# One tuned two-layer kernel on one core: the last x block turned by DMA, half-block closing, late statistics, one value product, and a new order of work

## The chip, the cores and the metric

The kernel runs on one core of a Trainium2 chip. The metric is device time in microseconds (us) of that core. A profile shows one execution; its span is about 2 us shorter than the device time of the same run.

Engines: PE is the matrix engine, DVE is VectorE, ACT is ScalarE, POOL is GpSimd.

## The reference

The same pair of blocks runs twice, on 2048 tokens of width 512. Block A is a spectral filter: a two-dimensional real FFT, a product with complex weights, the inverse. Block B is attention with 32 query heads of width 16 and one shared key and value head.

```python
def _A_ref(x, w_r, w_i):
    X = rfft2(x.astype(float32)); X = X * (w_r + 1j * w_i)
    return irfft2(X, s=(S, D)).astype(bfloat16)

def _B_ref(x, wq, wk, wv, wo):                  # H = 32, Dh = 16, one k and one v
    scores = einsum("bhqd,bkd->bhqk", q, k) * Dh ** -0.5
    o = einsum("bhqk,bkd->bhqd", softmax(scores), v)
    return o.transpose(0, 2, 1, 3).reshape(B, S, H * Dh) @ wo

x = A_x
x = x + _A_ref(layernorm(x), w_r, w_i);  x = x + _B_ref(layernorm(x), wq, wk, wv, wo)
x = x + _A_ref(layernorm(x), w_r, w_i);  x = x + _B_ref(layernorm(x), wq, wk, wv, wo)
```

Written as matrix products with host-made tables, a layer has three phases in the trace: transposed blocks and a column transform, then the filter, then the inverse transform with normalization and keys and values (together the spectral stage), and then the attention.

## The kernel before

The kernel is a list scheduler in Python that runs when the program is built. It keeps a clock for each engine, books a duration for every task, and always emits the action that can start first. The instruction order of each engine is thus fixed before the chip sees it; the engines then only wait for each other.

```python
class Plan:
    ACT_EXP = 908.0; DVE_P1 = 600.0; DVE_PH = 610.0; POOL_PH = 1030.0; POOL_LAG = 2600.0   # booked ns
    def step(self):
        while True:
            for i in self.script.get(self.acts, ()):     # choices forced by SCRIPT, by action number
                self.turns.add(i)
            best = None
            for e, c in zip(self.t, (self.pe_next(), self.act_next(), self.dve_next(), self.pool_next())):
                if c is not None and (best is None or c[0] < best[0]):
                    best, eng = c, e
            ...
```

`SCRIPT` is a packed list of small forced choices: at action number n, take the second candidate of an engine, hold PE a little, or put the pass named below on the other engine. It is the "order". As it goes by action number, an edit that adds or removes tasks shifts everything after it, which matters for reading two of the experiments.

In attention, a score unit is 128 keys by 512 queries of one head. ACT takes units in pairs and computes exact exponentials. DVE takes single units: one scale-and-round pass from the PSUM bank to 16-bit integers (below: a score pass), after which two more integer additions per four units (below: phase passes) complete the approximate exponential. A phase pass goes to GpSimd, or, if GpSimd's queue is over 2.6 us long or the order says so, to DVE:

```python
def close(self, end):
    ...
    for p in range(1, K_PH):
        if last: ...
        elif (max(self.t["POOL"] + self.POOL_PH * len(self.pool), end) - end < self.POOL_LAG) != ("phase" in self.turns):
            self.pool.append(...)          # GpSimd: int64_add on the packed 16-bit values
        else:
            self.ph_fifo.append(...)       # DVE: one integer addition, 128x2048
```

The parts that the change touches: statistics aggregate at once, the normalization has a separate shift, each of four value copies is its own instruction, and a block of queries closes only when its last two head groups are normalized together.

```python
def bn(self, L, key, i, x, n, slot=None):
    ...
    self.nc.vector.bn_stats(st, self.ps(slot) if slot else self.x[:, x[1], x[0], :])
    self.nc.vector.bn_aggr(mv[:, i, :], st)

def v_evac(self, t, slot):
    src = self.ps(slot)[:, 0:64].rearrange("p (r d) -> p r d", r=R)
    for i, v in enumerate(self.VS):                        # 1 + 3 weighted copies
        dst = v[:, 4 * t:4 * t + 4, 0:DH]
        if i == 0:
            self.nc.vector.tensor_copy(out=dst, in_=src)
        else:
            self.nc.vector.tensor_single_scalar(out=dst, in_=src, scalar=self.pw[i - 1], op=ALU.mult)

def done(self, b, slot, end):                              # an attention block is finished
    ...
    rc = p.add("DVE", 260.0, [ev, self.evac[b - 1]], lambda k: em.recip(self, b), lazy=tail)
    mu = p.add("DVE", 600.0, [rc], lambda k: em.mul(self, b), lazy=tail, port=True)
    ...                                                    # last two blocks: transposed by DVE, others by DMA
    if g == 3:
        self.layer.close_rows(qb, ...)                     # projection, new x, next layer's statistics
```

The softmax here doesn't subtract the row's maximum and nothing guards it: scores larger than these inputs give would overflow.

## Time and profile before

| | before |
|---|---|
| device time, median of 6 runs | 1315.18 us (1313.65 to 1315.22) |
| profiled span | 1312.7 us |
| first transpose of x on PE | 7.01 us |
| first, third filter group on DVE (see below) | 33.35, 44.64 us |
| DVE score passes, first layer | 108.10 to 663.91 us |
| third filter group, second layer | 695.65 us |
| DVE score passes, second layer | 758.98 to 1301.29 us |

The times of the score passes are the start of the first and the end of the last.

Start with the page: busy time of each engine (share of the span, number of instructions), and for DVE and ACT the span in 40 slices of 33 us, each digit the busy share in tenths. ACT and DVE are full in the attention slices; the two spectral stages are the dips of ACT at the left and in the middle.

```profile
...
PE 1281.5 (98%) x12986; PEld 433.1 (33%) x12986; DVE 1272.7 (97%) x2277; ACT 1223.3 (93%) x1397; POOL 840.1 (64%) x825
...
DVE  6999999999999999999979999999999999999998
ACT  6488999999999999999954899999999999999996
...
```

The DVE alone, from the third filter group to the first score pass of each layer: busy for 58.8 of 63.5 us, so this stage is limited by DVE too, with 4.7 us of waits.

```profile
...
44.64:108.10 63.46, 58.80 (x158) 1.00 0.07 22
695.65:758.98 63.33, 58.61 (x159) 1.00 0.07 22
...
```

The timeline of DVE at the end of the first spectral stage (columns: start us, length us, engine, line, operation, output and input tiles, shapes; in brackets the idle time in front and what ended it). A statistic starts at 98.25, its aggregate at 98.97 and the next work at 99.07. The last aggregate starts at 101.16, the first apply (the instruction that normalizes a row) 0.99 us later. The four value copies start from 106.84 to 107.23. DVE waits 0.60 us for ACT, then 1.24 and 0.66 us for PE.

```profile
...
98.25 0.69 DVE L1091 BATCH_NORM_STATS2 st<-x_sb 128x6 f32<-128x512 bf16 x1
98.97 0.18 DVE L1092 BATCH_NORM_AGGREGATE mv<-st 128x2 f32<-128x6 f32 x1
99.07 0.66 DVE L1317 TENSOR_TENSOR x_sb<-b_68,x_sb 128x512 bf16<-128x512 f32 x1
...
101.16 0.18 DVE L1092 BATCH_NORM_AGGREGATE mv<-st 128x2 f32<-128x6 f32 x1
101.94 0.17 DVE L1108 SCALAR_TENSOR_TENSOR sb<-mv,sb 128x4 f32<-128x4 f32 x1 [0.60 <-ACT sb L1104]
102.15 1.38 DVE L1115 TENSOR_SCALAR xnt<-x_sb,sb 128x512 bf16<-128x512 bf16 x4
...
106.17 0.75 DVE L1348 TENSOR_SCALAR KA<-b_68,part 128x512 bf16<-128x512 f32 x1 [1.24 <-PE b_68 L1340]
106.84 0.22 DVE L1360 CAST vs_116<-b_67 128x64 bf16<-128x64 f32 x1
...
107.23 0.22 DVE L1362 TENSOR_SCALAR vs_119<-b_67 128x64 bf16<-128x64 f32 x1
108.10 0.69 DVE L1394 TENSOR_SCALAR w_1381<-b_68 128x512 uint16<-128x512 f32 x1 [0.66 <-PE b_67 L1382]
...
```

The timeline of PE at the head: matrix products on zeros run until 6.80 us, and the first transpose is at 7.01.

```profile
...
5.00 0.63 PE L1073 MATMUL b_67<-zero 128*128 128x512 bf16 x1
5.43 0.45 PE L1073 MATMUL b_68<-zero 128*128 128x512 bf16 x1
...
6.80 0.38 PE L1073 MATMUL b_66<-zero 128*128 128x512 bf16 x1
7.01 0.61 PE L1152 MATMUL b_67<-tab_ident,x_sb 128*128 128x128 bf16 x8
...
```

The layer change on DVE: the last score pass, the closing of the last block, and the statistics of four new rows one after the other.

```profile
...
663.23 0.68 DVE L1394 TENSOR_SCALAR w_9868<-b_68 128x512 uint16<-128x512 f32 x1
...
666.18 0.72 DVE L1411 STREAM_TRANSPOSE raw<-b_69 128x512 f32<-128x512 f32 x1 [0.70 <-PE b_69 L1404]
...
669.75 0.70 DVE L1091 BATCH_NORM_STATS2 st<-b_67 128x6 f32<-128x512 f32 x1 [0.99 <-PE b_67 L1310]
...
673.23 0.67 DVE L1091 BATCH_NORM_STATS2 st<-b_69 128x6 f32<-128x512 f32 x1
...
684.71 1.29 DVE L58 TENSOR_TENSOR w_10097<-w_9940 128x1024 bf16<-128x1024 bf16 x2 [2.83 <-ACT w_9940 L1216]
```

### The profile page before, as it was taken

What the parts mean: (1) busy time and instruction counts of PE and PEld (TensorE: products, weight loads), DVE (VectorE), ACT (ScalarE), POOL (GpSimd) and SP (SyncE); (2) the same over time, 40 slices, a digit from 0 to 9 for tenths busy, and PEclk for the clock granted to TensorE, in tenths of its full rate; (3) what the DMA queues carried; (4) which work ended last, traced back from release to release, by engine and by line L of the source; (5) the groups of instructions that cost most, each with busy time, mean ns of one, the idle gap of its engine ahead of it and who ended that gap; (6) DMA issues with size and microseconds to landing.
All of it is one profiled execution on the core that took longest, in us unless ns stands there. A gap on an engine that the chain in (4) does not pass through costs nothing.

```text
span 1312.7 us, 31767 instructions
## 1 busy us (share of the span) xinstructions
PE 1281.5 (98%) x12986; PEld 433.1 (33%) x12986; DVE 1272.7 (97%) x2277; ACT 1223.3 (93%) x1397; POOL 840.1 (64%) x825
## 2 busy tenths in 40 slices
PE   9999999999999999999999999999999999999997
PEld 5642222322232222222256423232222232233222
DVE  6999999999999999999979999999999999999998
ACT  6488999999999999999954899999999999999996
POOL 0005777767777677766720067787777777777775
PEclk9999999999999999999999999999999999999999
DMA  9100000011010100010051000000100010000101
GB/s 294 46 1 1 10 9 10 9 32 19 2 12 12 36 10 10 9 34 17 10 169 41 1 1 9 10 10 9 22 14 10 9 22 14 5 8 11 27 5 25
DMA packets 108722, 33.04 MB, mean 25 GB/s; under 512 B 88352, under 2 KB 107296, under 8 KB 108576
## 3 DMA queue, kind: packets, MB, share of 16 engines
q1 hardware_dynamic: 108288, 30.46, 10.0%
q8 instruction: 101, 1.65, 0.5%
q10 hardware_dynamic: 288, 0.56, 0.1%
q14 instruction: 45, 0.37, 0.1%
HBM read 17.89 MB, written 7.60 MB: 19 GB/s over the span
## 4 chain that ended last, share of the span: by engine, by line
ACT 72%; PE 18%; DVE 10%; issue 1%; DVEq 0%
ACT e_0_84 L1387 3%; ACT e_10_94 L1387 3%; ACT e_13_97 L1387 3%; ACT e_3_87 L1387 3%; ACT e_20_104 L1387 3%; ACT e_4_88 L1387 3%; ACT e_12_96 L1387 3%; ACT e_2_86 L1387 3%; ACT e_8_92 L1387 3%; ACT e_7_91 L1387 3%; ACT e_11_95 L1387 3%; ACT e_18_102 L1387 3%; ACT e_1_85 L1387 3%; ACT e_5_89 L1387 3%; ACT e_15_99 L1387 3%; ACT e_14_98 L1387 3%
## 5 line engine op out<-in xcount | busy, mean ns | idle before, releaser
L1382 PEld LDWEIGHTS <-KB 32*128 32x128 bf16 x2048 | 89.7, 91 | 228.5 <-issue 221.4
L1382 PEld LDWEIGHTS <-KA 32*128 32x128 bf16 x2048 | 86.4, 91 | 238.4 <-issue 231.5
L1404 PEld LDWEIGHTS <-vs_116 128*32 128x32 bf16 x2474 | 99.9, 94 | 93.0 <-issue 87.9
L1404 PEld LDWEIGHTS <-vs_117 128*32 128x32 bf16 x1622 | 96.0, 94 | 64.0 <-issue 60.5
L1404 PEld LDWEIGHTS <-vs_118 128*32 128x32 bf16 x1622 | 70.6, 94 | 70.5 <-issue 65.9
L1404 PEld LDWEIGHTS <-vs_119 128*32 128x32 bf16 x1622 | 68.4, 94 | 64.8 <-issue 61.4
L1398 POOL INT64_ADD w_1382<-w_1381 x1 | 1.0, 1040 | 108.1 <-DVE w_1381 L1394 108.1
L1398 POOL INT64_ADD w_10977<-w_10976 x1 | 1.0, 1038 | 97.2 <-DVE w_10976 L1394 97.2
L1387 ACT ACTIVATE e_6_90<-sa_64 128x1024 bf16<-128x1024 f32 x34 | 39.8, 1172 | 1.0 <-PE sa_65 L1382 1.0
L1091 DVE BATCH_NORM_STATS2 st<-x_sb 128x6 f32<-128x512 bf16 x52 | 35.4, 682 | 4.0 <-DMA x_sb<-in_A_x_dram 3.6
L1387 ACT ACTIVATE e_11_95<-sa_65 128x1024 bf16<-128x1024 f32 x31 | 36.5, 1178 | 0.7 <-PE sa_65 L1382 0.7
L1387 ACT ACTIVATE e_12_96<-sa_65 128x1024 bf16<-128x1024 f32 x31 | 36.9, 1189 | 0.2 <-PE sa_65 L1382 0.2
L1387 ACT ACTIVATE e_2_86<-sa_64 128x1024 bf16<-128x1024 f32 x31 | 36.5, 1178 | 0.4 <-PE sa_64 L1382 0.4
L1387 ACT ACTIVATE e_4_88<-sa_65 128x1024 bf16<-128x1024 f32 x31 | 36.6, 1182 | 0.1
L1387 ACT ACTIVATE e_1_85<-sa_64 128x1024 bf16<-128x1024 f32 x31 | 36.6, 1180 | 0.1
L1387 ACT ACTIVATE e_7_91<-sa_64 128x1024 bf16<-128x1024 f32 x31 | 36.6, 1181 | 0.0
L1387 ACT ACTIVATE e_15_99<-sa_65 128x1024 bf16<-128x1024 f32 x31 | 36.6, 1179 | 0.0
L1387 ACT ACTIVATE e_20_104<-sa_65 128x1024 bf16<-128x1024 f32 x31 | 36.4, 1175 | 0.0
L1387 ACT ACTIVATE e_13_97<-sa_64 128x1024 bf16<-128x1024 f32 x31 | 36.2, 1168 | 0.0
L1387 ACT ACTIVATE e_14_98<-sa_65 128x1024 bf16<-128x1024 f32 x31 | 36.0, 1162 | 0.0
L1387 ACT ACTIVATE e_0_84<-sa_65 128x1024 bf16<-128x1024 f32 x30 | 35.5, 1183 | 0.2 <-PE sa_65 L1382 0.2
L1387 ACT ACTIVATE e_9_93<-sa_64 128x1024 bf16<-128x1024 f32 x30 | 35.1, 1170 | 0.2 <-PE sa_64 L1382 0.2
(4077 smaller groups left out, 6474.8 us busy)
## 6 DMA issues: line engine op xcount, KB each, us to landing
it<-const_IT SPq DMA_DIRECT2D x8, 640.0 KB, 5.6
onw<-on SPq DMA_DIRECT2D x120, 32.0 KB, 1.9
x_sb<-in_A_x_dram SPq DMA_DIRECT2D x4, 512.0 KB, 6.8
out_dram<-x_sb SPq DMA_DIRECT2D x16, 128.0 KB, 1.9
way<-x_sb SPq DMA_DIRECT2D x6, 256.0 KB, 2.2
tab_PH<-const_PH ACTq DMA_DIRECT2D x1, 512.0 KB, 4.9
w_131<-const_FT SPq DMA_DIRECT2D x1, 512.0 KB, 8.8
w_136<-const_FT SPq DMA_DIRECT2D x1, 512.0 KB, 8.4
```

The lines of the kernel that those rows point to most:

```text
L1091: self.nc.vector.bn_stats(st, self.ps(slot) if slot else self.x[:, x[1], x[0], :])
L1382: self.nc.tensor.matmul(o, lhsT=KX[rs, kc * P:(kc + 1) * P], rhs=at.QT[qb][rs, g, :], start=True, stop=True, skip_group_check=True)
L1387: self.wrote("ACT", e, self.nc.scalar.activation(out=e, in_=self.ps(slot), func=ACT.Exp, scale=SCALE))
L1398: self.nc.gpsimd.int64_add(t[p][:, 0:n].bitcast(U64), t[0][:, 0:n].bitcast(U64), DELTA[p] * FOUR)
L1404: self.nc.tensor.matmul(self.ps(slot)[32 * h:32 * h + 32, :], lhsT=V[:, kc, :], rhs=rhs, start=first, stop=last, skip_group_check=True)
```

## The change

The intent is to shorten what is not attention, and to let the last queries of a layer close in two halves, so that part of the layer change runs while attention still fills the engines.

1. The plan knows when x arrives, and the last of the four x blocks comes turned by DMA straight from the input, without PE transposes and ACT copies.
2. The statistics of a tile are aggregated one tile late, the shift of the normalization folds into its apply, and the four value copies become one product with broadcast weights.
3. The last token block is normalized in two row pairs, (0, 2) and (1, 3), and so is the first, which before had the pairs (0, 1) and (2, 3).
4. The last two attention blocks of a layer each take both head parities of half of the queries, so rows 0 and 1 can close while rows 2 and 3 attend.
5. A new `SCRIPT`, with one more kind of choice ("flex": ACT may take evacuations that either engine can do while DVE attends).

```diff
-SCRIPT = ( "0ax00902q00k05h..." )
+SCRIPT = ( "1dm02i02d00g00x..." )                         # cut
@@ Layer
+    DMA_X = {3: 13000.0}
+    PAIRED = (0, 3)
@@ load_x
+        for t in L.DMA_X:
+            for j in range(0, R, 2):
+                self.turned(L, [(t, j), (t, j + 1)], self.xt_v[t, P * j:P * j + 2 * P, :])
@@ bn
-        self.nc.vector.bn_stats(st, ...)
-        self.nc.vector.bn_aggr(mv[:, i, :], st)
+        late.append((i, self.small([6], "st", 8)))
+        self.nc.vector.bn_stats(late[-1][1], ...)
+        L.bn_left[key] = L.bn_left.get(key, n) - 1
+        for j, st in late[:] if L.bn_left[key] == 0 else late[:-1]:
+            self.nc.vector.bn_aggr(L.sb[key][0][:, j, :], st)
+            late.pop(0)
@@ apply
-        self.nc.vector.tensor_scalar(..., scalar1=sb[:, 0, i:i + 1], scalar2=sb[:, 1, i:i + 1], op0=ALU.mult, op1=ALU.add)
+        self.nc.vector.tensor_scalar(..., scalar1=mv[:, i, 0:1], scalar2=sb[:, 0, i:i + 1], op0=ALU.subtract, op1=ALU.mult)
@@ v_evac
-        for i, v in enumerate(self.VS): ...               # four copies
+        self.nc.vector.tensor_tensor(out=self.vs[:, :, 4 * t:4 * t + 4, 0:DH], in0=src.unsqueeze(1).to_broadcast(shape),
+                                     in1=self.vw.to_broadcast(shape), op=ALU.mult)
@@ add_back: output rows
-            for j in range(0, R, w): ... for i, r in enumerate(range(j, j + w)):
+            for rows in ((0, 2), (1, 3)) if t in self.PAIRED else (...): ...
@@ Attention
+        self.halves = {nb - 2: 0, nb - 1: 1}
@@ scores
+            if b in at.halves:
+                q = 256 * at.halves[b]
+                for i, KX in enumerate((self.KA, self.KB)):
+                    self.nc.tensor.matmul(o[:, 256 * i:256 * i + 256], lhsT=KX[rs, ...], rhs=at.QT[qb][rs, g, q:q + 256], ...)
+                continue
@@ done
+        if b in self.halves:
+            ...                                            # normalize 256 queries, then
+            self.layer.close_rows(qb, ..., (2 * hf, 2 * hf + 1))
```

Cut here: booked durations, the bookkeeping of the halves and pairs, and the packed order itself.

## The prediction

> **What bounds the kernel now.** Time before: 1315.18 us; profiled span 1312.7 us. Stages in the windows view:
> - Attention, 115-660 and 767-1300 us, 82% of the span: per 20 us ACT is busy 19.9-20.0, DVE 19.5-20.0, GpSimd about 15.5. Score units are shared: 0.917 us of ACT per two units (start to start), 0.60 us of DVE per unit, together 3.85 units/us. A microsecond of DVE work here is worth 0.43 us, of ACT 0.57 us.
> - First spectral stage, 0-108 us. Its head is a chain x, transpose, ACT copy, product, ACT scaling, DVE radix steps; from 33 to 107 us DVE is the limit (18.8-19.6 of 20).
> - Layer change, 664-759 us: the same, entered through the projection of the last rows.
> - Tail, 1301.4-1312.7 us.
>
> **What the change moves.**
> 1. Head. x is there at 4.77 us (first statistics), but PE transposes at 6.80 us, behind dummy matmuls that start every 0.43 us until 5.4 us, then every 0.22 us (as the Trainium skill, "TensorE: Matmul & The Clock Gate", Part 1, gives for cold and warm). The new plan knows this: -1.8 us. Turning the last x block by DMA removes two transposes of 0.45 us and two ACT copies of 0.9 us. Against it, DMA share is 1.0-1.2 until 22 us, and a later DMA transpose of this size takes 3.1-3.7 us to land; weights come later, but not too late. The first filter (33.35 us) should start 2.5-3.5 us earlier.
> 2. DVE in both spectral stages. Statistics now cost 0.79-0.80 us a tile because the aggregate waits for its own tile; one tile late saves about 0.11 us, 16 times per stage after 33 us: 1.7 us. Four value copies take 0.52 us per block, one product an estimated 0.33: 0.8 us. The shift (0.15 us, 5 per stage) goes: 0.7 us. Sum 3 us on a DVE-limited chain, twice.
> 3. Last token block in pairs: at 101-108 us DVE idles 0.6, 1.24 and 0.66 us. Pairs should win 1-1.5 us, twice.
> 4. Halves: the last two blocks each take half of the queries, so rows 0 and 1 close while rows 2 and 3 attend. At the layer change two first products (0.87 us each), a transposition pair, two statistics and half of the normalization leave 666-679 us: 4-5 us shorter, but about 2.6 us of ACT and 2 us of DVE move into attention, costing about 2.4 us. Net -2. Tail: half normalization -1.1 us, two additions fewer -1.2, part paid back: -1.8 us. Score matmuls become twice 256 columns; those start every 0.11 us, so PE should not care.
> 5. New order: attention is full already, about 0.
>
> Sum: head -3, DVE -6, pairs -2.4, layer change -2, tail -1.8, attention -0.5: -15.7 us; I discount it a little.
>
> **Predicted: 1301 us, 8 in 10 between 1293 and 1310.** Faster by over 2%: 0.07; within 2%: 0.91; slower by over 2%: 0.02.
>
> **What would show it.** First transpose near 5 us; first filter near 30 us; first DVE score pass near 100 us instead of 108.1; the gap between last and first DVE score pass at the layer change 95 -> about 86 us; tail 2 us shorter; attention windows unchanged.
>
> **What would make it wrong.** DMA transposes landing after 20 us or delaying filter weights; halves starving the score banks, so that ACT or DVE idles in the last blocks; savings that turn into PE waits; a new order that packs worse.

## More of the kernel before

A filter group is DVE's work on one set of transformed columns: additions of the transform, the product with the complex weights, and more additions. The groups serve as milestones in both traces; the first is dated by its first addition, the third by its first product.

Next the busy time of the engines in the two attention stretches, from the first to the last DVE score pass (columns: stretch, its length, then busy us and number of instructions of each engine, TensorE clock, DMA share, GB/s). DVE is busy 552.51 of 555.81 us and ACT 554.82: an attention stretch has two full engines and no slack.

```profile
...
core 0: us, PE busy (x) PEld busy (x) DVE busy (x) ACT busy (x) POOL busy (x), PEclk, DMA share, GB/s
108.10:663.91 555.81, 548.04 (x5754) 162.58 (x5754) 552.51 (x941) 554.82 (x615) 414.54 (x408) 1.00 0.09 17
758.98:1301.29 542.31, 534.92 (x5726) 159.62 (x5726) 540.42 (x903) 541.51 (x592) 421.16 (x406) 1.00 0.07 12
...
```

## The result and the profile after

| | before | after |
|---|---|---|
| device time, median of 6 runs each | 1315.18 us (1313.65 to 1315.22) | 1307.79 us (1307.62 to 1307.81) |
| ratio | | 0.9946, 95% interval 0.9933 to 0.9959 |
| profiled span | 1312.7 us | 1305.9 us |

A ratio is the mean time of one kernel's fast runs over that of the other's of the same rounds, so it is not quite the ratio of the medians quoted. The change is 7.4 us (0.5%) faster, the class is "same within 2%"; the time is inside the predicted range and 6.8 us above the predicted value. Only 7.4 of the 15.7 us of the prediction's sum came, so the range held by its width (1310 was its upper end), not because the sum was right. The kernel before varies by 1.6 us from run to run, so differences of less than that between two single profiles are weak evidence alone.

The milestones of the two traces cut the span into seven stretches. I use the third filter group, not the first, to end the head; the reason is given below.

| stretch | before | after | difference | predicted |
|---|---|---|---|---|
| head, to the third filter group | 44.64 | 41.46 | -3.18 | -3 |
| first spectral stage, to the first score pass | 63.46 | 61.90 | -1.56 | -4.2 |
| attention 1 | 555.81 | 559.60 | +3.79 | +1.9 for both |
| layer change, to the third filter group | 31.74 | 28.48 | -3.26 | -4.4 |
| second spectral stage | 63.33 | 60.09 | -3.24 | -4.2 |
| attention 2 | 542.31 | 544.77 | +2.46 | (see above) |
| tail | 11.41 | 9.60 | -1.81 | -1.8 |
| span | 1312.70 | 1305.90 | -6.80 | -15.7 |

In the last column the sums of the prediction are laid on the stretches: DVE -3 and pairs -1.2 for each spectral stage; the halves as -4.4 in the layer change and +2.4 in attention, against which the -0.5 stood.

The attention stretches are again full on both engines, but longer. DVE does 4.24 us more work in the first (556.75 against 552.51), GpSimd 6.24 us less (408.30 against 414.54). That hides a shift: ACT runs 599 and 595 score exponentials in the two stretches, against 597 and 592 before, and DVE 804 and 812 score passes against 806 and 816. At 0.917 us from start to start (measured before), two and three more exponentials are 1.8 and 2.8 of the 3.4 and 3.2 us by which ACT's busy time grew. One of them in each stretch is there because ACT had begun 24 exponentials, not 25, before DVE's first score pass.

```profile
...
103.36:662.96 559.60, 548.43 (x5850) 164.74 (x5881) 556.75 (x951) 558.25 (x618) 408.30 (x398) 1.00 0.09 17
751.53:1296.30 544.77, 535.02 (x5819) 163.76 (x5844) 541.98 (x906) 544.69 (x595) 415.35 (x400) 1.00 0.07 12
...
```

Part of what DVE does more is phase passes that the new order gives to it. This is their share of the same two stretches (count in brackets); the kernel before has none there.

```profile
...
103.36:662.96 559.60, 6.48 (x8) 1.00 0.09 17
751.53:1296.30 544.77, 2.75 (x4) 1.00 0.07 12
...
```

A phase pass on DVE has no fixed price. Among the 14 of this kernel, those of 128x2048 16-bit values that began with GpSimd quiet took 0.68 to 0.70 us (the tier table of the Trainium skill's "VectorE: DVE Perf Modes" has 693 ns for such an instruction on bf16 values, which agrees). Two took 1.24 us, each begun while a GpSimd addition had 0.7 us left to run, and two took 1.58 us, begun together with one. The Trainium skill, "GPSIMD Engine Reference", § 1, Specifications, says that GpSimd shares SBUF interfaces with VectorE and that they contend with DVE instructions in a 2-port mode. The trace agrees that they contend: in each of the four cases DVE seems to wait out the running GpSimd instruction (1.04 us) and then take 0.55 us. The two timelines of the kernel after around such a case, DVE first (GpSimd's first addition began at 405.57, 0.34 us ahead; its line is two additions merged):

```profile
...
405.91 1.24 DVE L1471 TENSOR_SCALAR w<-w 128x2048 uint16<-128x2048 uint16 x1
...
```

```profile
...
405.57 2.48 POOL L1469 INT64_ADD w<-w  x2 [2.91 <-DVE w L1465]
...
```

DVE from the third filter group to the first score pass: busy time fell by 2.1 us in the first stage (58.80 to 56.67) and by 2.3 us in the second. The waits (length minus busy) went from 4.66 to 5.23 us in the first and from 4.72 to 3.75 us in the second.

```profile
...
41.46:103.36 61.90, 56.67 (x141) 1.00 0.08 23
691.44:751.53 60.09, 56.34 (x143) 1.00 0.08 23
...
```

The end of the first spectral stage. The aggregates no longer wait, four copies became one product of 0.42 us. The pairs removed one of the three waits: the first apply now follows the last aggregates at once (97.27), and the 0.60 us for ACT are gone, because ACT makes the second pair's factors while DVE applies the first pair's. In the second layer the same wait of 0.60 us is gone too. The two waits for PE stayed (1.46 and 0.70 us against 1.24 and 0.66). PE did not get the first pair any earlier: DVE took the second pair's statistics first and then ran all four applies in one go.

```profile
...
97.05 0.30 DVE L1150 BATCH_NORM_AGGREGATE mv<-st 128x2 f32<-128x6 f32 x2
97.27 1.35 DVE L1169 TENSOR_SCALAR xnt<-x_sb,mv,sb 128x512 bf16<-128x512 bf16 x4
...
101.43 0.75 DVE L1415 TENSOR_SCALAR KA<-b,part 128x512 bf16<-128x512 f32 x1 [1.46 <-PE b L1407]
102.24 0.42 DVE L1425 TENSOR_TENSOR vs<-b,vw 128x256 bf16<-128x256 f32 x1
103.36 4.59 DVE L1465 TENSOR_SCALAR w<-b 128x512 uint16<-128x512 f32 x7 [0.70 <-PE sa L1453]
...
```

ACT in the same time: the last step to each pair's factors. The first pair's were ready at 95.61, 1.66 us before DVE used them; the second pair's at 97.82, inside the applies.

```profile
...
95.40 0.20 ACT L1163 ACTIVATE sb<-sb 128x2 f32<-128x2 f32 x1
...
97.62 0.20 ACT L1163 ACTIVATE sb<-sb 128x2 f32<-128x2 f32 x1
...
```

The head: the first transpose is at 4.77 us, where x arrives.

```profile
...
2.42 2.34 PE L1128 MATMUL b<-zero 128*128 128x512 bf16 x5
4.77 1.70 PE L1219 MATMUL b<-tab_ident,x_sb 128*128 128x128 bf16 x16
...
```

The layer change. One row got its statistics at 656.01, inside attention. The second row got them at 664.56, after the last score pass; the last two followed (the first of them at 668.49), and the third filter group was reached 28.48 us after the last score pass instead of 31.74.

```profile
...
656.01 0.69 DVE L1147 BATCH_NORM_STATS2 st<-b 128x6 f32<-128x512 f32 x1
...
663.06 1.57 DVE L1471 TENSOR_SCALAR w<-w 128x2048 uint16<-128x2048 uint16 x1
664.56 0.68 DVE L1147 BATCH_NORM_STATS2 st<-b 128x6 f32<-128x512 f32 x1
...
668.49 0.70 DVE L1147 BATCH_NORM_STATS2 st<-b 128x6 f32<-128x512 f32 x1 [0.75 <-PE b L1377]
...
680.45 1.29 DVE L58 TENSOR_TENSOR w<-w 128x1024 bf16<-128x1024 bf16 x2 [2.54 <-ACT w L1283]
...
```

**Why the third filter group.** At the first filter group the gain of the head is 4.04 us (33.35 to 29.31). From the first middle product on, however, PE runs without a gap, and the filter groups wait for its products: ACT began the copy of the product that the third group needs at 43.60 before and at 40.42 after, 3.18 us apart. DVE then waited 0.26 us for that copy before and 1.14 us after; the two lines of DVE, before and after:

```profile
...
44.64 1.23 DVE L1233 TENSOR_TENSOR w_598<-w_561,w_436 128x2048 bf16<-128x2048 bf16 x1 [0.26 <-ACT w_561 L1216]
...
```

```profile
...
41.46 2.36 DVE L1300 TENSOR_TENSOR w<-w,w 128x2048 bf16<-128x2048 bf16 x2 [1.14 <-ACT w L1283]
```

So 0.86 us of the early gain is turned into that wait, in a part of the stage that PE limits. In the second layer this doesn't happen: first and third group lie 10.94 us apart before and 10.99 after.

### The profile page after: what moved, and what is told of

Read it like the earlier page. It is cut to its first block, busy times and chain, and to the rows that moved or that the text cites. A ratio compares the mean times of both kernels' runs of the same rounds, so it can differ in the third digit from the quotient of the medians.

```text
span 1305.9 us, 32044 instructions
## 1 busy us (share of the span) xinstructions
PE 1270.4 (97%) x13113; PEld 436.0 (33%) x13187; DVE 1270.4 (97%) x2253; ACT 1224.8 (94%) x1402; POOL 828.2 (63%) x814
## 3 DMA queue, kind: packets, MB, share of 16 engines
q1 hardware_dynamic: 110400, 30.98, 10.4%
## 5 line engine op out<-in xcount | busy, mean ns | idle before, releaser
L1458 ACT ACTIVATE e<-sa 128x1024 bf16<-128x1024 f32 x1240 | 1143.7, 1163 | 6.9 <-PE sa L1453 6.1
L1469 POOL INT64_ADD w<-w x794 | 825.2, 1052 | 459.6 <-DVE w L1465 322.9
L1465 DVE TENSOR_SCALAR w<-b 128x512 uint16<-128x512 f32 x1616 | 990.2, 677 | 6.5 <-PE sa L1453 1.7
L1475 PE MATMUL b<-w,vs 128*32 128x512 bf16 x4848 | 537.6, 385 | 1.0 <-POOL w L1469 0.4
L1475 PE MATMUL b<-e,vs 128*32 128x512 bf16 x2480 | 420.8, 385 | 0.7 <-DVE w L1465 0.4
L1453 PE MATMUL sa<-w,KA 32*128 32x512 bf16 x1200 | 232.5, 381 | 9.0 <-ACT e L1458 6.7
L1453 PE MATMUL b<-w,KB 32*128 32x512 bf16 x792 | 236.7, 382 | 2.6 <-DVE w L1465 1.0
L1475 PEld LDWEIGHTS <-vs 128*32 128x32 bf16 x7328 | 141.1, 94 | 283.8 <-issue 267.6
L1453 PE MATMUL sa<-w,KB 32*128 32x512 bf16 x1128 | 222.6, 380 | 4.0 <-ACT e L1458 2.5
L1453 PE MATMUL b<-w,KA 32*128 32x512 bf16 x720 | 216.4, 382 | 2.7 <-ACT KB L1413 1.0
```

The source lines that it names most:

```text
L1453: self.nc.tensor.matmul(o, lhsT=KX[rs, kc * P:(kc + 1) * P], rhs=at.QT[qb][rs, g, :], start=True, stop=True, skip_group_check=True)
L1458: self.wrote("ACT", e, self.nc.scalar.activation(out=e, in_=self.ps(slot), func=ACT.Exp, scale=SCALE))
L1465: self.nc.vector.tensor_scalar(out=t[0][:, j], in0=self.ps(slot), scalar1=P1_SCALE, scalar2=P1_BIAS, op0=ALU.mult, op1=ALU.add)
L1469: self.nc.gpsimd.int64_add(t[p][:, 0:n].bitcast(U64), t[0][:, 0:n].bitcast(U64), DELTA[p] * FOUR)
L1475: self.nc.tensor.matmul(self.ps(slot)[32 * h:32 * h + 32, :], lhsT=V[:, kc, :], rhs=rhs, start=first, stop=last, skip_group_check=True)
```

## The experiments

Twelve kernels ran, all correct, in three batches; each batch ran on one chip with its own runs of the kernel before (medians 1314.58, 1314.13, 1314.71). The rival theories: (A) the DVE savings are real, but the new order packs attention worse, above all by the phase passes that it puts on DVE; (B) the DVE savings were turned into waits for PE and ACT and never reached the time; (C) the halves or the DMA turn took back in attention or in the head what they gave.

### Statistics aggregated at once

```diff
# on the kernel after
-        for j, st in late[:] if L.bn_left[key] == 0 else late[:-1]:
+        for j, st in late[:]:
```

> The kernel after, its order unchanged, but each aggregate follows its own statistics at once, as before. Theory 'the DVE savings count in full, the spectral stages being DVE-limited': about 0.11 us for 16 tiles in each of two spectral stages, so 3 to 4 us slower than after (1311 us). Rival theory 'the savings turned into waits on PE and ACT' (in the first spectral stage DVE busy time fell by 2.15 us, but its idle time rose by 1.45 us): under 1.5 us slower, about 1308.5 us.

Measured: 1312.14 us (1312.03 to 1312.30), ratio 0.9982 (0.9970 to 0.9995). Undoing the late aggregate alone takes 4.4 us of the 7.4. By the stretches: head +0.9, first spectral stage +1.0, attention 1 +0.9, second spectral stage +1.4, the rest within 0.2. In this order, one line of the change is more than half of its effect; it was undone with the order fixed, so this is not what it would be worth in an order made without it.

### All of the DVE part undone

```diff
# on the previous one
-        self.nc.vector.tensor_tensor(out=self.vs[...], in0=src..., in1=self.vw..., op=ALU.mult)
+        for i, v in enumerate(self.VS): ...               # the four copies of before
@@ apply
+        if key not in L.bn_shift:
+            L.bn_shift.add(key)
+            self.nc.vector.scalar_tensor_tensor(out=sb[:, 1, :], in0=mv[:, :, 0], scalar=-1.0, in1=sb[:, 0, :], op0=ALU.mult, op1=ALU.mult)
-        ... scalar1=mv[:, i, 0:1], scalar2=sb[:, 0, i:i + 1], op0=ALU.subtract, op1=ALU.mult
+        ... scalar1=sb[:, 0, i:i + 1], scalar2=sb[:, 1, i:i + 1], op0=ALU.mult, op1=ALU.add
```

> As the last one, and also the four value copies and the shift are back; again the order of after. 'Savings count in full': 3 us per spectral stage, so about 6 us slower than after (1314 us), nearly the whole gain lost. 'Turned into waits': 2 us slower or less (1309.5 us).

Measured: 1313.97 us (1313.88 to 1314.05), ratio 0.9996 (0.9984 to 1.0009): the kernel is back at the time of before. The DVE of this kernel, from the third filter group to the first score pass of each layer:

```profile
...
42.47:105.97 63.50, 59.41 (x160) 1.00 0.08 22
694.96:757.74 62.78, 58.95 (x160) 1.00 0.07 22
...
```

Against the kernel after, DVE is busy 2.74 and 2.61 us longer (59.41 and 58.95 against 56.67 and 56.34), near the 3 us a stage that I predicted. The stretches are 1.60 and 2.69 us longer. So (B) is wrong for the second stage and holds for about 1.1 us of the first. A second reading: with the DVE part undone, the first stage takes 63.50 us, as long as before (63.46), and the second 62.78 (63.33). All else that the change did to these stages, the pairs included, is then worth 0.0 and 0.55 us where I had counted 1.2 each. The end of the stage shows the pairs by themselves: from the start of the last statistic to the first score pass it is 7.64 and 7.73 us before and 6.89 us in both layers here, 0.75 and 0.84 less, with no wait for ACT. What took that back earlier in the stages (order, row order, the first block) no run separates.

### Phase passes back on GpSimd, order kept

```diff
# on the kernel after, in phase()
+        if eng == "DVE":
+            self.dve_passes = getattr(self, "dve_passes", 0) + 1
+            eng = "DVE" if self.dve_passes in (9, 14) else "POOL"   # 9 and 14: last units of a layer, as in before
```

> The kernel after, its order unchanged, but the 12 phase passes that its order puts on DVE inside the attention stretches (6.0 us in the first, 2.4 us in the second) are done by GpSimd. Theory 'DVE holds attention up in this order': 3 to 8 us faster (about 1302 us). Rival 'ACT is as full as DVE, and a fixed order can't move score units from ACT to DVE': within 1 us of after, or a little slower where a pass on GpSimd comes later.

Measured: 1306.19 us (1306.13 to 1306.54), ratio 0.9938 (0.9925 to 0.9950). That is some 1 us better than the kernel after (ratios 0.9938 and 0.9946, intervals overlap), 1.3 us of it in attention 1 by the profiles, which is nearer to the rival theory. 9.2 us of DVE work (6.48 + 2.75) left the attention stretches, and only 1.5 us came back as time: in the first, DVE's busy time fell to 552.47 us of 558.30.

```profile
...
103.29:661.59 558.30, 551.21 (x5880) 164.31 (x5881) 552.47 (x943) 557.82 (x618) 415.15 (x406) 1.00 0.09 17
...
```

The work was taken away, but the other instructions kept their order and each unit its engine, so DVE waits instead (5.83 us, against 2.85 in the kernel after). ACT is as full as it was (idle 0.5 us), so it sets the length.

### The same passes put on DVE in the kernel before

```diff
# on the kernel before, in phase()
+            self.pool_passes = getattr(self, "pool_passes", 0) + 1
+            eng = "DVE" if self.pool_passes in (2, 5, 218, 221, 233, 234, 336, 337, 403, 406, 517, 519) else "POOL"
```

> The kernel before, its order unchanged, but 12 phase passes at the places where after has them go from GpSimd to DVE. If work on a full DVE costs its whole time in a fixed order: 12 times 0.6 us, about 7 us slower than before (1322 us). If it costs what the balance of ACT and DVE says, 0.43 of that: about 3 us slower (1318 us). If there is slack: no change.

Measured: 1324.98 us (1322.96 to 1327.04), ratio 1.0081 (1.0067 to 1.0094): 10.4 us slower. The first eight passes make attention 1 longer by 5.3 us (561.14 against 555.81), the other four make attention 2 longer by 4.6 us (546.88 against 542.31). Here is the share of these passes in the two stretches, then the engines in them:

```profile
...
108.38:669.52 561.14, 7.09 (x8) 1.00 0.09 17
764.55:1311.43 546.88, 4.38 (x4) 1.00 0.07 12
...
```

```profile
...
108.38:669.52 561.14, 550.56 (x5754) 161.59 (x5755) 557.87 (x949) 556.44 (x615) 406.39 (x400) 1.00 0.09 17
764.55:1311.43 546.88, 536.91 (x5726) 159.34 (x5726) 543.97 (x907) 542.73 (x592) 417.14 (x402) 1.00 0.07 12
...
```

7.09 us of DVE work cost 5.3 us, and 4.38 cost 4.6. ACT did the same number of exponentials and stood idle for 4.7 and 4.2 us (length minus busy; 1.0 and 0.8 before). In a shared, balanced stretch I price a DVE microsecond at 0.43 us; that price needs an order that moves units over to ACT. With the order fixed, PE issues in the old sequence and everything waits with DVE. The price is also asymmetric: adding cost three quarters of its time or all of it, removing (the run before this one) gave little. More than the expected 12 times 0.6 us was added, because these passes took 0.89 and 1.10 us each on average.

### No DMA turn of the last x block

```diff
-    DMA_X = {3: 13000.0}
+    DMA_X = {}
```

> The kernel after without the DMA turn of the last x block: PE transposes and ACT copies it as before. The order's forced choices then fall on other actions, so only the head is to be compared, not the whole time. Theory 'the DMA turn is about half of the 4.0 us that the head won': first filter at about 31.3 us (after 29.31, before 33.35), first DVE score pass at about 105.4 us (after 103.36). Rival 'the earlier first transpose alone did it': first filter within 0.5 us of 29.3.

Measured: 1323.29 us, one run, state unknown. The total says nothing: the edit adds tasks in the head, so the order's action numbers no longer fit, and attention 1 took 571.45 us with 14 us of idle ACT. The head is read by itself: the first filter group came at 31.69 us (29.31 in the kernel after) and the third at 42.63 (41.46). The DMA turn is worth 2.4 us at the first group and 1.2 us at the third, where PE has become the limit. What is left at the first group without it, 1.66 us (33.35 to 31.69), is near the 1.8 us that the prediction gave to the earlier first transpose.

### No halves

```diff
-        self.halves = {nb - 2: 0, nb - 1: 1}
+        self.halves = {}
# and the closing of the last two blocks as in before: one normalization by DVE, statistics in pairs of rows
```

> The kernel after with the last two attention blocks as before (by head group, all queries, closed together). Its order is that of after up to the last blocks of the first layer, so only the end of that layer and the layer change are to be compared. Theory 'the halves cost attention little and shorten the layer change, though only one of the four rows gets its statistics early': last DVE score pass 1 to 2 us earlier than in after (662.96), but from there to the first filter 20.8 us as before instead of 17.5 us; net, first DVE score pass of layer 2 about 2 us later than in after (751.53). Rival 'the halves' own cost in attention eats their gain': net within 0.5 us.

Measured: 1324.49 us, one run, state unknown. Here the action numbers fit until the first layer closes, so attention 1 and the layer change can be read (attention 2, 557.05 us, can't). Attention 1 is 557.59 us, 2.0 shorter than with halves, with the same eight passes on DVE; the layer change to the third filter group is 31.99 us, 3.5 longer. I had predicted 2.4 and 4 to 5, net -2; the net is -1.5. The halves do what they should, a little less: only one of four rows had its statistics inside attention.

### No order at all, before and after

```diff
-SCRIPT = ( "..." )
+SCRIPT = ""
```

> The kernel before without its list of forced choices (an empty order string: the list scheduler's own first choice everywhere). Theory 'both kernels owe a large part of their time to their order': 15 to 30 us slower than before, about 1338 us.

> The kernel after, also without its list of forced choices. Theory 'the parts of the change are worth more than 7 us, and the new order gives some of it back': at least 8 us faster than the plain kernel before, and about 20 us slower than after (1327 us). Rival 'the parts are worth the measured 7 us or less, whatever the order': 3 to 7 us faster than the plain kernel before. A plain order scatters by some us with any change, so this pair alone settles it only if it is far to one side.

Measured: before without an order 1332.49 us (1332.36 to 1332.63), ratio 1.0140 (1.0123 to 1.0157); after without one 1322.29 us (1322.26 to 1322.65), ratio 1.0063 (1.0048 to 1.0078). Between the two lie 10.2 us, not 7.4. The order that each kernel came with is worth 18.4 us in the kernel before (1332.49 against that batch's 1314.13) and 14.5 us in the kernel after (1322.29 against 1307.79, another chip).

### Both kernels with an order from one short search

The same search for both: the scheduler is run forward, small sets of forced choices are tried every few dozen actions, and the set with the least booked time is kept; best of three starts, neither "phase" nor "flex" allowed. Its booked times chose the order and are evidence of nothing else.

```diff
-SCRIPT = ( "..." )
+SCRIPT = ( "..." )                                        # from the search, for each kernel
```

> The kernel after with another order: a new list of forced choices from a search with three starts, which may not choose 'phase' (so no pass goes to DVE inside attention). Theory 'the parts are worth about 10 us when both kernels get orders of the same quality, and after's own order is only as good as this short search': within 2 us of after (1307.5 us), while the kernel before from the same search (next run) is 9 to 12 us slower than this one. Rival 'the parts are worth 7 us': the two searched kernels are 6 to 8 us apart.

> The kernel before with an order from the same search, same three starts and same number of tries. Theory 'before's own order was the better tuned one': 4 to 6 us slower than before with its own order (about 1319 us).

Measured: after 1307.97 us (1307.87 to 1308.03), ratio 0.9949 (0.9937 to 0.9962); before 1318.87 us (1318.11 to 1319.31), ratio 1.0031 (1.0019 to 1.0044). With equal care for the order the parts are worth 10.9 us. Each order is one draw, though: how much the result of such a search scatters was not measured. The search reached what the kernel after came with, and missed what the kernel before came with by 4.2 us. Laid on the stretches (after minus before, us, one profile of each):

| stretch | predicted | orders as they came | both searched | both without |
|---|---|---|---|---|
| head | -3 | -3.18 | -3.64 | -4.33 |
| first spectral stage | -4.2 | -1.56 | -3.23 | -3.06 |
| attention 1 + 2 | +1.9 | +6.25 | +2.07 | +5.89 |
| layer change | -4.4 | -3.26 | -2.36 | -3.29 |
| second spectral stage | -4.2 | -3.24 | -1.99 | -3.02 |
| tail | -1.8 | -1.81 | -2.25 | -2.28 |
| span | -15.7 | -6.8 | -11.4 | -10.1 |

### A kernel from what was learned

The kernel after, its order kept up to the second attention, that stretch searched anew without "phase", and the first eight DVE passes given to GpSimd.

```diff
-SCRIPT = ( "..." )
+SCRIPT = ( "..." )                                        # kept up to the choice at action 4390, then from the search
@@ phase
+        if eng == "DVE" and ... the first eight: eng = "POOL"
```

> The version meant to beat both: after with its order kept up to the second attention stretch, the rest searched again, and the eight phase passes that its order puts on DVE in the first attention stretch done by GpSimd (which won 1.3 us before). Expected 1305.5 us, about 2 us faster than after. If the second stretch gains nothing on the chip: 1306.2 us, as the run with passes on GpSimd.

Measured: 1306.62 us (1306.59 to 1306.73), ratio 0.9939 (0.9926 to 0.9953). It beats the kernel before, and the kernel after by about 1 us at overlapping intervals; it is no better than the run with all passes on GpSimd. The new second stretch gained nothing (544.88 us against 544.77), with two passes on DVE instead of four. So the passes are not what makes attention 2 longer.

### The order planned anew from 375 us on

```diff
-SCRIPT = ( "..." )
+SCRIPT = ( "..." )                                        # kept up to the choice at action 2158, then from the search, without "phase"
```

> After with its order kept to about 375 us and the rest searched again without choosing passes on DVE, so the units are shared out again between ACT and DVE (this the run with the same order and passes on GpSimd could not do). Theory 'passes on DVE cost 0.43 us a microsecond': first attention stretch (559.6 us in after, six of its eight passes, 4.8 us of DVE, gone) about 2 us shorter. Rival 'the search had chosen them because they fill gaps, and they cost little': within 1 us of 559.6 us, or of the 558.3 us with passes on GpSimd.

Measured: 1307.54 us (1307.39 to 1308.08), ratio 0.9947 (0.9934 to 0.9959). Attention 1 is 557.17 us, 2.4 shorter than in the kernel after; six of its eight DVE passes are gone and the two early ones remain. Attention 2 is 0.9 us longer and the second spectral stage 1.5 (from the first filter group), so the total didn't move.

```profile
...
103.62:660.79 557.17, 549.06 (x5873) 164.83 (x5874) 553.29 (x945) 556.83 (x617) 412.62 (x404) 1.00 0.09 18
...
```

Compare this row, attention 1, with the kernel after: DVE is busy 553.29 instead of 556.75 us, GpSimd 412.62 instead of 408.30, and the stretch is shorter by 2.4 us, where the fixed order gave 1.3 for more work taken away. This run changes everything after 375 us, not the passes alone.

## Why the prediction was right or wrong

**Right: the head, the tail, and what limits each stretch.** The first transpose moved from 7.01 to 4.77 us (predicted near 5), and the tail shrank by 1.81 us (predicted 1.8). At the milestone that the prediction named, the first filter group, the head gained 4.04 us, more than the predicted 2.5 to 3.5; 0.86 us of that became a wait for PE, and at the third group 3.18 us are left. I chose the third group after seeing the traces, so its match with the predicted 3 is partly luck. The spacing of the PE's zero products before, 0.43 and then 0.22 us, agrees with what the Trainium skill, "TensorE: Matmul & The Clock Gate", Part 1, gives for the cold and the warm clock.

**Right in kind, a little too large: DVE, "Sum 3 us on a DVE-limited chain, twice".** Undoing it added 2.74 and 2.61 us of DVE work and 1.60 and 2.69 us of time in the two stages, and 6.2 us in all (1313.97 against 1307.79 on another chip), because it also shows in the head and in attention 1. The late aggregate alone is 4.4 us of this. The Trainium skill, "VectorE: DVE Perf Modes", "The DRAIN you can't avoid", says that an instruction that reads what the one before it wrote needs a semaphore or an instruction in between; no run here shows a stale read, but the price of having no instruction between was 0.12 us a tile (medians: 0.72 us from a statistic to its own aggregate before, 0.60 us to the next instruction after). The value product was sized well: estimated at 0.33 us (a straight line through the trace before, 0.13 us for 64 columns and 0.60 us for 512, gives this), measured at 0.31 to 0.34 us start to start where the next instruction did not wait.

**Too large: "Pairs should win 1-1.5 us, twice".** I had counted on all three waits at the stage's end (0.6, 1.24 and 0.66 us). The pairs took away the first, for ACT, in both layers; the two for PE stayed. DVE ran both pairs' applies in one go, so PE got the first pair no earlier, which is probably why; no run tested it. With the DVE part undone, the stage's end was 0.75 and 0.84 us shorter than before, but the whole stages took 63.50 and 62.78 us against 63.46 and 63.33, so of the counted 2.4 us only 0.55 are seen there. No run had the pairs alone, so what took the rest back is open.

**Too large: the layer change, "4-5 us shorter".** It was 3.26 us shorter, because only one row was ready inside attention. The cost in attention (2.0 us) and so the net (-1.5) were close to the prediction.

**Wrong: "New order: attention is full already, about 0."** This is the step that failed in kind. I took "full" to mean that an order can't make it better or worse, although "a new order that packs worse" stood in my list of what would make the prediction wrong. The stretches grew by 6.25 us instead of 1.9, although both engines stayed as full as before: ACT had two and three more exponentials to do, DVE twelve phase passes. With an equal search for both kernels the same parts cost 2.07 us in attention, close to the prediction. With no order in either they cost 5.89 there, with idle engines in both, and won more elsewhere; so how much of a stretch is parts and how much order depends on the order, and only the totals are firm. Those say: the parts give 10.2 us (no orders) or 10.9 us (equal search), the change as made 7.4. So the order before seems to fit its parts better than the new one fits its own, and this took back some 3 us (2.8 or 3.5). The two comparisons agree, but each rests on one pair of orders whose scatter is not known.

One cause inside the new order is shown: eight phase passes on DVE in attention 1 (6.48 us of DVE). Moving them with the order fixed gave 1.3 us there; planning anew with two of them, which changes the rest of the order too, gave 2.4 us. With the 2.0 us of the halves, which were predicted, the 1.3 us leave 0.5 of that stretch's 3.79 us open. In the second attention moving all four passes gave 0.2 us, and there the cause isn't settled: before's own order runs that stretch in 542.31 us, and the same parts with the searched order take 544.29. The kernel after with the searched order has 816 score passes on DVE again and no phase pass, and takes 544.96 us, so the units moved to ACT are not the whole cause either.

The difference from the prediction's sum, 15.7 less 7.4 or 8.3 us, is thus two things of like size: some 3 us that a worse-fitting order seems to have taken back, and about 5 us of parts counted too large. Of these the profiles show 4.7: 1.9 of the 2.4 counted for the pairs, 1.1 of the layer change, and 1.7 of the 6 counted for the DVE part (1.4 of it in the first stage).

## What to carry to other kernels

When both kernels come with tuned orders, a difference of them mixes the parts with the tuning: compare them also with no order and with an equal search, before you judge a part. "Engines are full" does not make an order neutral, since they can be full with work that another engine had room for. A fixed order prices work one-sidedly: added work on a full engine cost most of its time or all of it (7.09 us cost 5.3, 4.38 cost 4.6), while removed work gave back 1.5 of 9.2 us, since the other engine was just as full. Planned anew, the first stretch gave back 2.4 us, but the total, 1307.54 us, was no better than the 1306.19 with the order kept.

## What the Trainium skill lacked or had wrong

- "VectorE: DVE Perf Modes" has no durations for the statistics instructions, and no other page has them. Here one on 128x512 took 0.63 to 0.70 us and its aggregate 0.15 to 0.18 us; where nothing else held it, the next instruction started 0.69 to 0.73 us after a statistic if it was its own aggregate and 0.55 to 0.62 us after it if it was not.
- "DMA: Bandwidth & Descriptors", § Latency and other measured facts, gives an effective bandwidth for DMA transposes, and no latency of one under load. Here two transposes from the input landed 6.5 us (median) after their issue in the crowded head, and six of the same size later landed after 3.2 us.
- No page says what a fixed instruction order does to the price of work; the two runs that moved the phase passes (+10.4 us for adding 12 of them, -1.6 us by the medians and about -1 us by the ratios for removing 12) are the numbers.
